# One held PSUM slot for both heads, an earlier start, earlier weights and an even product rate in a fused attention and feed-forward kernel

## The chip, the cores and the metric

The kernel runs on one core of a Trainium2 chip. The metric is the device time of one execution in microseconds (us). Engines are named as in the profile: PE (TensorE), DVE (VectorE), ACT (ScalarE), POOL (GpSimd), SP (the engine whose queue issues most transfers). A span is the time from the first to the last instruction of the profiled execution; an execution takes about 1.8 us more than its span (325.73 against 323.9 us). Each run also lists the mean clock that PE was granted (0.983 to 1.0 here), and that turns out to matter.

## The reference, cut to what matters

```python
# B, H, S, D = 4, 8, 768, 64; proj: 64 x 6
mask   = bucket(q) == bucket(k)          # six sign bits of q @ proj and k @ proj
scores = where(mask, q @ k.T / 8, -1e9)
attn   = softmax(scores) @ v             # per batch and head
x      = attn as (3072, 512)
h      = x @ w_in                        # 512 -> 2048
g      = h + sin(alpha * h)**2 / alpha
out    = g @ w_out                       # 2048 -> 512
```

There are 16 pairs of heads, four to a batch. A pair takes 12 steps: two heads, six blocks of keys.

## The kernel before

The parts that the change touches. `slot()` hands out two-bank pieces of PSUM in rotation, three in all; scores use them, and a slot taken with `hold=True` leaves two to the scores. Banks 6 and 7 hold the weighted values and the product of the last matrix.

```python
turns = deque(range(3))
def slot(hold=False):
    n = turns.popleft()
    if not hold:
        turns.append(n)
    return banks[:, 2 * n:2 * n + 2, :], n
```

A pair's q and k are prepared in parts during the pair ahead of it. For the first six pairs PE makes the transposed blocks:

```python
def prepare_on_pe(i):
    ...                                   # copies, hash, bits, picks; a yield after each part
    for h in range(2):
        if held is not None:
            give_back(held)
        ps, held = slot(hold=True)        # each head takes a slot
        for t in range(2):                # q, then k
            out = ps[0:KA, t, 0:HALF].bitcast(BF16)
            for s in range(SB):
                nc.tensor.transpose(out[:, s * 128:(s + 1) * 128], nat[:, s, 2 * t + h], ident)
            ...                           # DVE copies it out (once: ACT)
            yield
```

A step of attention issues the scores of one block of keys, its exponential on ACT, then `at_step` (parts of preparation, loads, product), then weighs by the values a block three steps old. When a head is weighed to its end, DVE computes `total`, a reciprocal and `xn` from bank 6, and from pair 5 on the next head weighs into the same bank.

```python
def fill(rate, most=3):                   # put some matmuls of the last product here
    nonlocal owed, rest
    owed += rate
    if rest:                              # the step after a finished tile places none,
        rest = False                      # while DVE copies the tile out of bank 7
        return
    while owed >= 1.0 and todo and most:
        owed -= 1.0
        most -= 1
        done = next(todo[0], None)        # one matmul; true if it finished a tile of 16
        if done is None:
            todo.popleft()
        if done:
            rest = True
            break
```

A batch is followed, one pair later, by its expansion (`x @ w_in`, sine, square: 16 chunks). Its product (96 matmuls, six tiles of 16) is then spread by `fill` over the four pairs that follow.

The softmax here doesn't subtract the row's maximum and nothing guards it: scores larger than these inputs give would overflow.

## Time and profile before

| what | before |
|---|---|
| runs known at the start | 326.29, 328.03 and 446.79 us (the last was the first execution) |
| median in the later calls, 9 to 11 runs each | 325.96 to 327.2 us |
| span of the profiled execution | 323.9 us |
| PE busy, ACT busy | 305.0 us (94%), 242.9 us (75%) |
| period of an early pair | 10.62 us |

### The profile page before, as it was taken

To read this page: it belongs to the slowest core of one execution; us is meant where nothing else is said; L and a number is where in the kernel's file an instruction comes from. 1 tells how busy PE (TensorE), PEld (TensorE's weight loads), DVE (VectorE), ACT (ScalarE), POOL (GpSimd) and SP (SyncE) were. 2 spreads that over 40 slices of the span, in tenths; PEclk is the share of its full clock that TensorE was granted. 3 is DMA by queue.
4 is the path that set the end of the run, shared out by engine and by line. 5 is a ranking of instruction groups with operands and counts; after the bars stand their busy time and mean duration, and the time that the engine had idled before them with its cause. 6 is when DMAs were issued, how large, how long until landed. Compare 5 with 4: busy or idle time off the path is not lost.

```text
span 323.9 us, 7681 instructions
## 1 busy us (share of the span) xinstructions
PE 305.0 (94%) x3059; PEld 183.3 (57%) x3059; DVE 196.7 (61%) x338; ACT 242.9 (75%) x298; POOL 94.6 (29%) x175
## 2 busy tenths in 40 slices
PE   6799999998989999989999999989999999899996
PEld 5566566664635556556645555656645655465444
DVE  4656546569864265569984466569984342499511
ACT  1387888888977778789988778789988888399200
POOL 5952642812883405051400605052300000000000
PEclk9799999999999999999999999999999999999999
DMA  7902576279965766869006476978003312200022
GB/s 257 328 4 60 183 235 191 72 207 257 376 235 144 159 172 152 232 109 200 0 2 195 113 213 106 223 125 192 2 9 92 66 71 59 57 2 0 4 113 81
DMA packets 68724, 42.87 MB, mean 132 GB/s; under 512 B 46560, under 2 KB 63696, under 8 KB 68688
## 3 DMA queue, kind: packets, MB, share of 16 engines
q1 hardware_dynamic: 68576, 42.37, 49.5%
q8 instruction: 24, 0.39, 0.5%
q14 instruction: 12, 0.10, 0.1%
q10 hardware_dynamic: 112, 0.01, 0.0%
HBM read 28.01 MB, written 7.27 MB: 109 GB/s over the span
## 4 chain that ended last, share of the span: by engine, by line
PE 66%; DMA 12%; DVE 6%; ACT 5%; POOL 5%; SPq 4%; issue 2%; ACTq 0%; DVEq 0%; POOLq 0%
PE banks L414 21%; PE banks L449 19%; PE banks L380 12%; PE banks L360 7%; ACT e L387 4%; PE banks L191 3%; PE banks L255 2%; DMA v_3064<-in_v_dram 2%; DMA k_150<-in_k_dram 2%; DMA v_3276<-in_v_dram 2%; SPq L92 2%; SPq L279 2%; DMA w_1467<-in_moe_w_in_dram 2%; DMA v_1090<-in_v_dram 1%; DMA w_1611<-in_moe_w_out_dram 1%
## 5 line engine op out<-in xcount | busy, mean ns | idle before, releaser
L387 ACT ACTIVATE e<-banks 128x768 bf16<-128x768 f32 x192 | 149.9, 810 | 36.7 <-PE banks L380 29.4
L449 PE MATMUL banks<-w_out_bf,g 128*128 128x512 bf16 (+1 forms) x400 | 102.1, 370 | 1.9 <-POOL w_out_bf L174 1.5
L380 PE MATMUL banks<-qa,ka 76*128 76x384 bf16 x384 | 94.2, 327 | 1.7 <-ACT e L387 1.4
L414 PE MATMUL banks<-xt,w_in_bf 128*128 128x384 bf16 x512 | 85.5, 326 | 2.2 <-POOL w_in_bf L174 1.2
L360 PEld LDWEIGHTS <-e 128*128 128x128 bf16 x1152 | 57.6, 97 | 35.4 <-issue 6.7
L414 PEld LDWEIGHTS <-w_in_bf 128*128 128x128 bf16 x512 | 49.5, 98 | 35.8 <-POOL w_in_bf L174 2.0
L360 PE MATMUL banks<-vaug,e 128*128 128x65 bf16 x1152 | 64.9, 193 | 2.0 <-DVE total L328 1.9
L423 ACT ACTIVATE s<-banks,alpha_sb 128x768 bf16<-128x768 f32 x64 | 57.2, 893 | 11.7 <-PE banks L414 10.9
L449 PEld LDWEIGHTS <-g 128*128 128x128 bf16 x400 | 38.7, 97 | 35.5 <-issue 3.7
L457 DVE COPY osb<-banks 128x512 f32<-128x512 f32 (+1 forms) x25 | 16.7, 668 | 30.4 <-PE banks L449 30.4
L328 DVE TENSOR_TENSOR total<-banks,base 128x390 f32<-128x390 f32 x20 | 11.2, 561 | 36.8 <-PE banks L360 36.7
L380 PEld LDWEIGHTS <-ka 76*128 76x128 bf16 x384 | 26.9, 99 | 6.1 <-issue 3.1
L208 POOL TENSOR_TENSOR vacc<-vacc,vaug 128x130 f32<-128x130 f32 x48 | 20.7, 431 | 3.8
L255 PE MATMUL banks<-ident,nat 128*76 128x128 bf16 x144 | 12.5, 231 | 4.2 <-ACT e L387 2.4
L255 PEld LDWEIGHTS <-nat 128*76 128x76 bf16 x144 | 11.0, 123 | 8.6 <-issue 3.7
L191 PE MATMUL banks<-qt,w_hash 128*32 128x192 f32 x128 | 13.7, 332 | 0.8 <-DVE qt L182 0.8
L191 PE MATMUL banks<-kt,w_hash 128*32 128x192 f32 x128 | 13.5, 332 | 0.3 <-DVE kt L182 0.3
L334 DVE TENSOR_TENSOR xn<-total,rden 128x384 bf16<-128x384 f32 x20 | 11.9, 597 | 0.7
L259 DVE COPY qa<-banks 76x768 bf16<-76x768 bf16 x12 | 6.6, 550 | 8.7 <-PE banks L255 8.7
L288 DVE TENSOR_SCALAR bits<-banks,side 128x192 bf16<-128x192 f32 x20 | 7.4, 412 | 5.5 <-ACT e L387 4.7
L191 PEld LDWEIGHTS banks<-qt,w_hash 128*32 128x32 f32 x128 | 6.0, 109 | 7.0 <-ACT e L387 2.5
L232 DVE TENSOR_SCALAR bit<-banks,bound 128x192 bf16<-128x192 f32 x6 | 2.5, 418 | 8.5 <-PE banks L191 8.5
(276 smaller groups left out, 290.5 us busy)
## 6 DMA issues: line engine op xcount, KB each, us to landing
out_dram<-osb SPq DMA_DIRECT2D x23, 256.0 KB
rows<-bits SPq DMA_DIRECT2D x40, 24.0 KB
w_663<-in_moe_w_in_dram SPq DMA_DIRECT2D x1, 512.0 KB
w_883<-in_moe_w_in_dram SPq DMA_DIRECT2D x1, 512.0 KB
w_1104<-in_moe_w_in_dram SPq DMA_DIRECT2D x1, 512.0 KB
w_1341<-in_moe_w_in_dram SPq DMA_DIRECT2D x1, 512.0 KB
w_1414<-in_moe_w_in_dram SPq DMA_DIRECT2D x1, 512.0 KB
w_1451<-in_moe_w_in_dram SPq DMA_DIRECT2D x1, 512.0 KB
```

The lines of the kernel that those rows point to most:

```text
L191: nc.tensor.matmul(out=ps[32 * j:32 * j + 32, 0:SB * 32].rearrange("p (s c) -> p s c", s=SB), lhsT=w_hash[:, blk].rearrange("p l a -> p (l ...
L208: nc.gpsimd.tensor_tensor(out=dst, in0=vacc[:, sb % 2], in1=vaug[:, :, sb], op=ALU.add)
L255: nc.tensor.transpose(out[:, s * 128:(s + 1) * 128], nat[:, s, 2 * t + h], ident)
L328: nc.vector.tensor_tensor(out=total, in0=cols, in1=operands[i][4][:, hh].unsqueeze(1).to_broadcast([128, SB, D + 1]), op=ALU.add,)
L334: nc.vector.tensor_tensor(out=xn[:, :, hh, :], in0=cols[:, :, 0:D], in1=rden.unsqueeze(2).to_broadcast([128, SB, D]), op=ALU.mult,)
L360: nc.tensor.matmul(out=regions[:, qb * (D + 1):(qb + 1) * (D + 1)], lhsT=e[:, qb * 128:(qb + 1) * 128], rhs=vaug[:, hh, kb, :], start=(apa ...
L380: nc.tensor.matmul(out=sc[:, half, 0:HALF], lhsT=ka[0:KA, hh, kb * 128:(kb + 1) * 128], rhs=qa[0:KA, hh, half * HALF:(half + 1) * HALF], s ...
L387: nc.scalar.activation(out=e.rearrange("p (h c) -> p h c", h=2), in_=sc[:, :, 0:HALF], func=AF.Exp, scale=SCALE,)
L414: nc.tensor.matmul(out=h[:, half, 0:HALF], lhsT=w_in_bf[:, p, F * 128:(F + 1) * 128], rhs=xt[b][:, p, half * HALF:(half + 1) * HALF], star ...
L423: nc.scalar.activation(out=s.rearrange("p (h c) -> p h c", h=2), in_=h[:, :, 0:HALF], func=AF.Sin, scale=alpha_sb[:, F:F + 1],)
L449: nc.tensor.matmul(out=o, lhsT=g[:, F, sub * 128:(sub + 1) * 128], rhs=w_out_bf[:, F, c0:c1], start=(F == 0), stop=(F == NF - 1),)
L457: nc.vector.tensor_copy(out=osb[:, c0:c1], in_=o)
```

## The change

Its intent: fewer waits of PE at each stage. The parts, as numbered in the prediction: (1) the start, (2) one held slot with steps moved by one, (3) weight pieces early, (4) an even product rate of 1.75, (5) a rate of 1.9 in the last three pairs.

```diff
         make_identity(nc, ident)
+        nc.gpsimd.tensor_copy(out=ident32, in_=ident[0:NF, 0:NF])           # (1)
 ...
-            for blk, engine in ((0, nc.vector), (1, nc.gpsimd)):
-                engine.tensor_copy(
+            for blk in range(2):
+                nc.gpsimd.tensor_copy(
                     out=w_hash[32 * a:32 * a + 32, blk, 0:NB, a], ...
     def invert_alpha():
-        nc.vector.tensor_copy(out=ident32, in_=ident[0:NF, 0:NF])
 ...
+        if held is not None:                                                # (2)
+            give_back(held)
+        ps, held = slot(hold=True)
         for h in range(2):
-            if held is not None:
-                give_back(held)
-            ps, held = slot(hold=True)
-            for t in range(2):
+            if (i, h) == (0, 1):
+                ps = banks[:, 6:8, :]
+            for t in ((1, 0) if i == 0 else (0, 1)):
 ...
-            at = [(0, n) for n in (1, 2, 4, 5, 7, 8, 8, 10)]
+            at = [(0, n) for n in (2, 3, 5, 6, 8, 9, 9, 11)]
-            at = [(i - 2, n) for n in (4, 7, 11)] + [(i - 1, n) for n in (1, 2, 3, 5, 6, 6, 8)]
+            at = [(i - 2, n) for n in (5, 7, 11)] + [(i - 1, n) for n in (1, 3, 4, 6, 7, 7, 9)]
 ...
-        for _ in range(3):                                                  # (1)
+        for _ in range(2):
             next(first)
         invert_alpha()
-        for _ in range(3):
+        for _ in range(4):
             next(first)
 ...
-                if n == 7 and 0 < i <= NPAIR:                               # (3)
-                    weigh_in(1 if i < NPAIR else 0)
-                fill(IN_ATTEND)                                             # was 2.0
+                if n in (8, 11) and 0 < i <= NPAIR:
+                    weigh_in(2)
+                fill(1.9 if i > n_pairs - NPAIR else 1.75)                  # (4), (5)
```

More of the change, by code (lines that the diff above doesn't have):

```diff
@@ L488, in drain @@
         owed, rest = 0.0, False
-    IN_ATTEND = 2.0
     n_pairs = len(pairs)
```

## The prediction

> **What bounds the kernel now.** I read the page first, then the times, then the waits of TensorE (PE) in total, then the timeline around each long one, and last the order of instructions of both kernels on each engine.
>
> The three runs are 446.79, 328.03 and 326.29 us. The first is far off and I drop it; the two others have a mean of 327.2, and the profiled execution took 325.73 with a span of 323.9. My base is 327.2.
>
> ```profile
> span 323.9 us, 7681 instructions
> PE 305.0 (94%) x3059; PEld 183.3 (57%) x3059; DVE 196.7 (61%) x338; ACT 242.9 (75%) x298; POOL 94.6 (29%) x175
> PE   6799999998989999989999999989999999899996
> PEclk9799999999999999999999999999999999999999
> ```
>
> PE is busy nearly everywhere, so it looks like the bound and leaves 324 - 305 = 19 us of idle time in all. But an early pair (the first five have no product to fill in) takes 10.6 us for 12 steps, and its steps without extra work follow each other in 0.51 us on PE (scores at 28.17 and 28.68); 12 x 0.51 plus the pair's hash, picks and 24 transposes (0.66 + 0.3 + 0.3 + 24 x 0.055) is some 8.7. In that part the 9s of the page are partly ends of matmuls that are only modelled, and stalls count more than the busy row says. The one low digit of the clock row is the slice at 8 to 16 us.
>
> The waits of PE, longest first:
>
> ```profile
> engine line waited for: us in total, times, longest us
> PE banks L255 <- ACT e L387: 2.4, 6, 0.4
> PE banks L360 <- DVE total L328: 1.9, 2, 0.9
> PE banks L449 <- POOL w_out_bf L174: 1.5, 3, 0.7
> ...
> PE banks L414 <- POOL w_in_bf L174: 1.2, 2, 0.7
> ...
> PE banks L153 <- DVE ident_105 L152: 1.2, 1, 1.2
> ...
> PE banks L414 <- DMA xt<-xn: 0.9, 1, 0.9
> ```
>
> Each of these six is a target of one part of the change; together 9.1 us. What the reader is to see: no single wait is large, and each sits in another stage. L255 is the block transposes, L360 the weighing by the values, L449 the last product, L414 the first product of the second half, L153 the transpose of alpha.
>
> The start, in order of time on VectorE (DVE), then on PE, then in the stretch from 11 to 12 us (busy time of PE, weight load, DVE, ACT and POOL, then the granted clock, 0.50, the DMA share and GB/s):
>
> ```profile
> 7.57 0.42 DVE L232 TENSOR_SCALAR bit<-banks,bound 128x192 bf16<-128x192 f32 x1 [0.95 <-PE banks L191]
> 7.90 0.78 DVE L152 CAST ident_105<-ident 16x16 f32<-16x16 bf16 x1
> 9.01 0.17 DVE L154 COPY alpha_sb<-banks 128x16 f32<-128x16 f32 x1 [0.32 <-PE banks L153]
> 9.21 0.49 DVE L155 TENSOR_SCALAR inv_alpha<-alpha_sb 128x16 f32<-128x16 f32 x1
> 9.74 0.25 DVE L156 RECIPROCAL inv_alpha<-inv_alpha 128x16 f32<-128x16 f32 x1
> 9.91 0.39 DVE L244 CAST nat<-banks 128x288 bf16<-128x288 f32 x1
> ```
> ```profile
> 10.46 2.55 PE L255 MATMUL banks<-ident,nat 128*76 128x128 bf16 x24 [1.23 <-POOL vaug L201]
> ```
> ```profile
> 11.00:12.00 1.00, 1.00 (x12) 1.00 (x11) 0.88 (x2) 0.23 (x1) 0.84 (x3) 0.50 1.08 378
> ```
>
> The bits are ready at 7.99, but four DVE instructions for alpha stand between them and the copy L244 that the transposes wait for; the picks on PE sit behind alpha's transpose too. The wait of L255 is put down to GpSimd (POOL); in program order that cast comes later, so it is L244. Then 24 transposes take 2.55 us, 106 ns each: the clock is at 0.50 from 11 to 14 us.
>
> [...] half clock for about three us, right after PE had been mostly idle from 7.5 to 10.4. [...] the 16x16 cast took 0.78 us and ended at 8.68, as the POOL cast that ran from 7.83 ended at 8.66; L155, 0.49 us for 16 columns, ended with the next POOL cast. [...]
>
> **The change part by part.** (1) Start. `ident32` is made by POOL beside the identity (near 1.5 us), alpha's transpose goes ahead of the hash on PE, and its three DVE instructions ahead of the bits, where DVE waited 0.95 for the hash. The eight copies into `w_hash` all go to POOL: 8 x 0.22 = 1.8 from 4.18, done at 6.0 in place of 5.07; DVE loses its four (0.70). The hash of k still needs k's transposed copy, bound by the landing of k near 5.7, so the hash ends near 7.4 as before. [...] bits start near 7.85, not 7.57. Then picks 8.3 to 8.6, L244 to 9.05, transposes at 9.15: 10.46 - 9.15 = 1.3 us earlier. The clock: half rate from 10.7 to 14 costs 3.3 / 2 = 1.6 us of PE's work; if the denser PE keeps the clock up it is saved. I give it 60%: 1.0. The casts of k for pair 1 land at 8.85 and stay ahead of need. Sum 2.3.
>
> (2) One held slot. Three slots of scores rotate and one is held. Before, the second head's transposes take another slot, whose exponential has to end first: in pair 2 PE waits 0.45 at 29.62 and 0.20 ahead of the next scores, then ScalarE (ACT) waits 0.63 for scores. Five pairs are prepared in this way during attention (1 to 5). Now head 1 uses head 0's slot, whose copies ended two steps (some 1.7 us) earlier. The first head still waits for a slot. 5 x 0.5 = 2.5, where 0.5 lies between PE's 0.45 and ACT's 0.63.
>
> (3) Eight weight pieces by pair 4 instead of four. The first expansion takes 67.14 to 91.1 us, 23.96, against 143.3 to 165.6, 22.3, for the second, which needs no weights. All eight pieces of the first matrix are loaded before it, the last two cast in its first two chunks; the eight of the second matrix follow in chunks of 1.4 us each at 1.4 us of transfer, done by chunk 11 of 16. Saves w_in 1.2 and w_out 1.5; but the first exponential after an expansion comes 4.59 us after its last matmuls start in both expansions, so part of w_out's wait is hidden: 2.4.
>
> (4) Product spread. 96 matmuls, 12 in the expansion, leave 84; at 2.0 a step they are used up with five steps left of 48. There PE runs 0.51 us steps and then stands 0.94 us for DVE's `total`, queued behind two stream transposes (1.9 us), once each in pairs 8 and 12. At 1.75, 84 / 48, the order of instructions shows two matmuls in the last step. A step with filler is 0.94 us, so the two steps between the DVE transposes and `total` cover them. 2 x (0.94 + 0.1 of small gaps) = 2.1.
>
> (5) Last batch. 1.9 instead of 2.0 over 36 steps: 16 matmuls, not 13, are left after the last weights, 3 x 0.215 = 0.65 against a wait of 0.94 for the last transposed block. 0.7.
>
> Sum 2.3 + 2.5 + 2.4 + 2.1 + 0.7 = 10.0. They lie in different stages on the path, so they add; I take off a tenth for what reappears as another small wait: 9.0. 327.2 - 9.0 = 318.2, put as 318.
>
> **The rivals.** (a) ACT becomes the bound of the early pairs. Against: its records follow each other 0.75 us apart (six in 4.51), 12 x 0.75 = 9.0 of 10.6. For: 12 x 0.81, the mean record, is 9.7, and with hash and picks on top part 2 would give 1 instead of 2.5: 320. (b) The start gains nothing: [...] the clock drops all the same: 320.5. Against: 1.3 us of DVE work leaves the path whatever the clock does. (c) Weight loads at steps 8 and 11 collide with the loads of q, k, v or POOL's casts, and an early pair waits: the DMA share is 0.33 to 0.64 from 30 to 66 us and POOL is busy about half, so four more casts of 1.04 us and 2 MB fit. If not, 1 to 3 us lost: 321. (d) An even spread leaves ACT short of scores instead: with 1.75 x 0.215 + 0.51 = 0.89 us a step PE stays slower than ACT's 0.81, so nothing is lost.
>
> **Range and chances.** Parts 3, 4 and 5 are read off as whole waits (5.2); 1 and 2 carry the doubt, 1.3 to 2.9 and 1 to 3. All low and a new wait gives about -6 (321.5); all high about -12.5 (314.5). 2% of 327.2 is 6.5, under the low end of most combinations: faster 0.85, same 0.14, slower 0.01.
>
> **What will show it.** Right: first transposes near 9.15 and first exponential before 12.2 (13.69 now); a clock row without the half-rate stretch (or with, then 1.6 worse); L255 waiting for ACT once, not six times, and early pairs of about 10.1 us; no waits for w_in; the first expansion near 22.3; no 0.94 wait for `total`; L414's wait for the last block gone. Wrong: pairs still 10.6 us with PE waiting for ACT elsewhere, POOL or the DMA queue ahead of PE in pairs 2 to 4, or DVE's `total` waits in other pairs.

## More of the kernel before

To compare stages I use the loads of ACT's function table, which part attention (exp) from expansion (sin). These are two of them in the timeline of ACT before; the columns are start, duration, engine, line and operation. Between them lies the second expansion, 23.37 us.

```profile
144.04 1.28 ACT L423 ACT_TABLE_LOAD   x1
...
167.41 1.28 ACT L387 ACT_TABLE_LOAD   x1
```

## The result, and the profile after

The median is 318.51 us (317.85 to 318.74, 4 runs) against 327.16 for the kernel before. The ratio is 0.9748, 95% interval 0.9698 to 0.9799. Ratios here are the mean time of one kernel's fast runs over that of the other's fast runs of the same rounds, so not quite the ratio of the medians. Executions over 1.5% slower than the fastest of the same kernel are left out of the means. A repetition (label e8_changed_again below) gave 318.85 and 0.9781. It was run at another time. The predicted time was 318.

The page after: span, busy time of the engines, PE's row and the row of its clock.

```profile
span 316.1 us, 7652 instructions
PE 301.7 (95%) x3029; PEld 184.3 (58%) x3059; DVE 196.0 (62%) x333; ACT 241.0 (76%) x298; POOL 94.4 (30%) x180
...
PE   7899999999999898999999899899999999999996
PEclk9999999999999999999999999999999999999999
```

The clock row has no low digit any more. The busy share of PE went from 94% to 95% and would not tell a reader that anything happened; it is also a little low after, where 30 records of the product are missing (x3029 against x3059). The waits of PE do (total us, times, longest):

```profile
PE banks L362 <- DVE total L330: 3.4, 4, 1.0
PE banks L382 <- ACT e L389: 1.1, 3, 0.4
...
PE banks L451 <- DVE osb L459: 0.6, 2, 0.3
...
PE banks L257 <- ACT e L389: 0.4, 1, 0.4
...
PE banks L416 <- DMA xt<-xn: 0.2, 1, 0.2
```

The waits for w_in and w_out are gone. The transposes (L257, which was L255) wait for ACT once instead of six times. The wait for the last transposed block fell from 0.9 to 0.2. But the wait for `total`, which part 4 was to remove, went up from 1.9 us in two places to 3.4 in four.

The table gives the length of each stage, worked out as differences of the start of the first exponential, of the table loads, of the first sine of the last expansion and of the span. Batches are named by the pairs in them.

| stage, us | before | after | difference | predicted, part |
|---|---|---|---|---|
| to the first exponential | 13.69 | 10.76 | -2.93 | -2.3 (1) |
| pairs 0 to 4 | 54.36 | 50.16 | -4.20 | -2.5 (2) |
| first expansion | 24.87 | 23.56 | -1.31 | -2.4 (3), with part of the next row |
| pairs 5 to 8 | 51.12 | 49.89 | -1.23 | and half of -2.1 (4) |
| second expansion | 23.37 | 23.74 | +0.37 | 0 |
| pairs 9 to 12 | 48.85 | 49.41 | +0.56 | half of -2.1 (4) |
| third expansion | 23.30 | 23.74 | +0.44 | 0 |
| pairs 13 to 15, to the last sine | 41.01 | 41.44 | +0.43 | -0.7 (5) |
| the rest | 43.33 | 43.40 | +0.07 | 0 |
| span | 323.9 | 316.1 | -7.8 | -10.0 before the deduction |

Each column is one trace. A second trace of the changed kernel (e8_changed_again) repeats the rows from pairs 5 on within 0.13 us, but its pairs 0 to 4 are 0.5 us longer and its first expansion 1.09 us longer (24.65), so the row of the first expansion is uncertain by about 1 us. And the 48.85 us of pairs 9 to 12 before is the lowest of all traces: four other kernels with the old rate have 49.28 to 49.41 there.

So the total came out as predicted while its terms did not. Two early ones gave more, and parts 4 and 5, for which I had counted 2.8 us of gain, show none. That is what the experiments are about.

My theory before them: the spread moves the step that rests after a finished tile. The order of instructions on PE in the changed kernel shows it. Here are steps 8 and 9 of pair 6 and steps 2 and 3 of pair 8; Q is the scores, cN are N product matmuls, V is the weighing, and the weighing of steps 9 and 3 is a head's first:

```
before:  pair 6, step 8   Q c3 V      step 9   Q c2 V
after:   pair 6, step 8   Q c1 V      step 9   Q    V      (rests)
before:  pair 8, step 2   Q c2 V      step 3   Q c2 V
after:   pair 8, step 2   Q c2 V      step 3   Q    V      (rests)
```

The same happens in pairs 10 and 12. These are the changed kernel's PE and DVE at step 3 of pair 8:

```profile
123.82 0.49 PE L382 MATMUL banks<-qa,ka 76*128 76x384 bf16 x2
125.18 0.34 PE L362 MATMUL banks<-vaug,e 128*128 128x65 bf16 x6 [0.87 <-DVE total L330]
```
```profile
123.84 0.69 DVE L459 COPY osb<-banks 128x512 f32<-128x512 f32 x1 [1.76 <-PE banks L451]
124.56 0.56 DVE L330 TENSOR_TENSOR total<-banks,base 128x390 f32<-128x390 f32 x1
```

A tile ended in the step in which a head ended. DVE copies the tile (0.69 us), then computes `total` (0.56 us). PE, with no product to place in this step, stands at the next head's first weighing, because it writes into the bank that `total` reads. The rival is that the spread is innocent and steps with a single product matmul (0.73 us in pair 6 of the changed kernel, from the scores at 100.53 us to the next at 101.26), shorter than ACT's exponential (0.81 us, the mean record), cost the time; or that its gain is there and hidden by something else.

### The profile page after: what moved, and what is told of

It is laid out like the page before. It is cut to its first block, busy times and chain, and to the rows that moved or that the text cites.

```text
span 316.1 us, 7652 instructions
## 1 busy us (share of the span) xinstructions
PE 301.7 (95%) x3029; PEld 184.3 (58%) x3059; DVE 196.0 (62%) x333; ACT 241.0 (76%) x298; POOL 94.4 (30%) x180
## 4 chain that ended last, share of the span: by engine, by line
PE 72%; DVE 9%; ACT 6%; DMA 5%; issue 3%; SPq 2%; POOL 1%; DVEq 0%; ACTq 0%; POOLq 0%
PE banks L416 23%; PE banks L451 19%; PE banks L382 15%; PE banks L362 9%; ACT e L389 4%; PE banks L191 3%; DVE g L403 3%; PE banks L257 2%; DMA v_3056<-in_v_dram 1%; DMA ka<-kn 1%; DMA k_145<-in_k_dram 1%; DVE total L330 1%; SPq L281 1%; ACT s L425 1%; DVE osb L459 1%
## 5 line engine op out<-in xcount | busy, mean ns | idle before, releaser
L389 ACT ACTIVATE e<-banks 128x768 bf16<-128x768 f32 x192 | 148.3, 811 | 33.8 <-PE banks L382 27.0
L451 PE MATMUL banks<-w_out_bf,g 128*128 128x512 bf16 (+1 forms) x370 | 98.1, 370 | 1.8 <-DVE osb L459 0.6
L425 ACT ACTIVATE s<-banks,alpha_sb 128x768 bf16<-128x768 f32 x64 | 57.1, 892 | 11.1 <-PE banks L416 10.2
L257 PEld LDWEIGHTS <-nat 128*76 128x76 bf16 x144 | 10.4, 114 | 3.6 <-issue 1.4
L257 PE MATMUL banks<-ident,nat 128*76 128x128 bf16 x144 | 11.5, 219 | 1.1 <-DVE nat L244 0.7
L201 POOL CAST vaug<-v_2847 128x768 bf16<-128x768 f32 x1 | 0.8, 830 | 25.4 <-DMA v_2847<-in_v_dram 25.4
```

The lines of the kernel that those rows point to most:

```text
L389: nc.scalar.activation(out=e.rearrange("p (h c) -> p h c", h=2), in_=sc[:, :, 0:HALF], func=AF.Exp, scale=SCALE,)
L425: nc.scalar.activation(out=s.rearrange("p (h c) -> p h c", h=2), in_=h[:, :, 0:HALF], func=AF.Sin, scale=alpha_sb[:, F:F + 1],)
L451: nc.tensor.matmul(out=o, lhsT=g[:, F, sub * 128:(sub + 1) * 128], rhs=w_out_bf[:, F, c0:c1], start=(F == 0), stop=(F == NF - 1),)
```

## The experiments

Twelve runs were made, one of them the changed kernel again; all were correct. "Before" is the kernel before on the same chip. By a threshold of 2% on the interval, e1, e7 and e9 to e12 are faster than before, e3 and e8 are unclear, and e2, e4, e5 and e6 count as the same; what they say about single parts rests on traces and on differences of a few us.

| run | median us | before | ratio (95% interval) |
|---|---|---|---|
| e1_rate_back | 316.41 | 327.2 | 0.9668 (0.9621 to 0.9715) |
| e2_rate_only | 327.41 | 327.2 | 0.9992 (0.9949 to 1.0034) |
| e3_slot_only | 320.21 | 327.2 | 0.9763 (0.9718 to 0.9807) |
| e4_start_only | 325.66 | 327.2 | 0.9909 (0.9835 to 0.9983) |
| e5_weights_only | 324.48 | 325.96 | 0.9949 (0.991 to 0.9987) |
| e6_steps_only | 323.51 | 325.96 | 0.9946 (0.989 to 1.0002) |
| e7_rest_moved | 317.23 | 325.96 | 0.9738 (0.9713 to 0.9762) |
| e8_changed_again | 318.85 | 325.96 | 0.9781 (0.9755 to 0.9808) |
| e9_tail_filled | 316.92 | 326.9 | 0.9686 (0.964 to 0.9732) |
| e10_even_but_last | 317.69 | 326.9 | 0.9708 (0.9662 to 0.9754) |
| e11_copy_on_act | 319.04 | 326.9 | 0.9745 (0.9694 to 0.9796) |
| e12_loads_earlier | 315.75 | 326.62 | 0.9671 (0.9639 to 0.9704) |

### The old rate in the changed kernel

```diff
-                fill(1.9 if i > n_pairs - NPAIR else 1.75)
+                fill(2.0)
```

> The changed kernel with only the rate of the product put back to 2.0 in every step. The prediction's parts 4 and 5 (the even spread saves 2.8) ask for 318.5 + 2.8 = 321.3. My theory after the two traces: the spread costs, because the step that rests after a finished product tile now falls on the first weighing of a head in pairs 6, 8, 10 and 12, and PE waits 3.4 us in all for DVE's total behind the copy of the tile, where the kernel before waited 1.9; the three stretches of pairs behind the expansions took 0.7, 1.0 and 0.4 us more than their share. It asks for 316.4, with two waits for total of 0.9 again and none of the four.

It took 316.41 us, where my theory had said 316.4 and the prediction's terms 321.3. Parts 4 and 5 cost about 2 us. The two old waits for `total` are back (1.9 us in two places), and so is the wait of 0.9 for the last block, and still it is faster than the changed kernel. The stages behind the pairs agree: 23.31 and 23.42 for the second and third expansion, 41.01 for the last pairs up to the sine. Pairs 5 to 8 take 49.33 instead of 49.89 us. Pairs 9 to 12 take 49.41 in both: here the old rate has a wait of 0.9 for `vsum`, a sum over v that POOL makes, in place of what it saves. PE's waits for ACT's exponentials are 1.1 us in three places in both kernels, which speaks against the rival of the short steps. The later repetition of the changed kernel, 318.85, keeps the distance; their ratios (0.9668 and 0.9781) stand apart. They were run at other times.

### The new rates in the kernel before

```diff
-                fill(IN_ATTEND)
+                fill(1.9 if i > n_pairs - NPAIR else 1.75)
```

> The kernel before with only the new rates. The prediction: 2.8 us faster than the kernel before. My theory: about 2 us slower, with four waits for total in pairs 6, 8, 10 and 12. A third view, that the spread costs only together with the faster early part, would give no difference.

The median is 0.2 us above that of before, ratio 0.9992: no gain, which refutes the term, but it does not show the 2 us of loss either. The waits are the ones of the theory:

```profile
PE banks L360 <- DVE total L328: 3.5, 4, 1.1
```

The stages behind the first expansion are longer by 0.48, 0.37, 0.66, 0.43 and 0.43 us in its trace, 2.4 together. The timed runs show less. Part of the gap goes with the clock: nine of the eleven runs of before had a mean clock of 0.983 to 0.995; of the six runs of this kernel, two had 1.0 and three 0.993 to 0.995, and the sixth, at 0.984, took 331.81 us and counts as slow. Among runs at 0.993 to 0.995, three of this kernel took 327.08 to 327.55 and two of before 326.09 and 326.82, some 0.8 us apart. So the size of the loss on this side stays between 0 and 2.4 us.

### The slot alone

Only part 2 of the diff, on the kernel before.

> The kernel before with only the one held slot and its shifted steps. The prediction gave 2.5 us for it (0.5 a pair). The traces say 4.2 for the five pairs (10.6 to 9.6 us each in the steady ones), so 4 to 5 us faster if the slot alone does it; 2.5 if half of it came from the start or from the weights.

It took 320.21 us, 7.0 below the median of before: most of the whole change. In the trace pairs 0 to 4 take 50.05 us instead of 54.36, 4.3 less (4.9 less than the 54.94 of the new rates on the old slots, a trace without a half-rate stretch). The rest of the difference of the medians goes in part with the clock: all four runs had 1.0, against 2 of 11 of before at 0.999 or above. To see where the 4.3 comes from, look at ACT in an early pair. First the kernel before, then the changed kernel (the slot alone gives the same lines at other times); in brackets is ACT's idle time before the group:

```profile
30.90 4.51 ACT L387 ACTIVATE e<-banks 128x768 bf16<-128x768 f32 x6 [0.63 <-PE banks L380]
35.81 2.22 ACT L387 ACTIVATE e<-banks 128x768 bf16<-128x768 f32 x3 [0.40 <-PE banks L380]
38.37 0.81 ACT L387 ACTIVATE e<-banks 128x768 bf16<-128x768 f32 x1 [0.34 <-PE banks L380]
39.38 1.51 ACT L387 ACTIVATE e<-banks 128x768 bf16<-128x768 f32 x2 [0.20 <-PE banks L380]
```
```profile
31.63 9.02 ACT L389 ACTIVATE e<-banks 128x768 bf16<-128x768 f32 x12 [0.58 <-PE banks L382]
```

Twelve exponentials run in one piece of 9.02 us, and one bubble of 0.58 us is left of four that summed to 1.57. The period is 9.02 + 0.58 = 9.60 us, against 10.62 (from 30.90 to the next group of six at 41.52). The early pairs are paced by ACT: each bubble of ACT counts in full, 1.57 - 0.58 = 0.99 us a pair. The gap of 0.63 us came back in every early pair of the kernel before, as a head took a second slot (before the groups at 21.50, 30.90, 41.52, 52.14 and 62.76 us), and is not in the changed kernel's piece above.

### The shifted steps alone

```diff
-            at = [(0, n) for n in (1, 2, 4, 5, 7, 8, 8, 10)]
+            at = [(0, n) for n in (2, 3, 5, 6, 8, 9, 9, 11)]
-            at = [(i - 2, n) for n in (4, 7, 11)] + [(i - 1, n) for n in (1, 2, 3, 5, 6, 6, 8)]
+            at = [(i - 2, n) for n in (5, 7, 11)] + [(i - 1, n) for n in (1, 3, 4, 6, 7, 7, 9)]
```

> The kernel before with only the steps of the preparation shifted, each head still in its own slot. The slot with its shift was worth 1.0 us a pair, 7 us in the median, where I had predicted 0.5 and 2.5. If the exchange of slots is the cost, this gives nothing; if a part comes from the shift, 1 to 3 us. The half-rate stretches that the kernel before shows in most runs should stay if the shift alone does nothing.

```profile
35.35 5.29 ACT L387 ACTIVATE e<-banks 128x768 bf16<-128x768 f32 x7 [0.58 <-PE banks L380]
41.27 3.80 ACT L387 ACTIVATE e<-banks 128x768 bf16<-128x768 f32 x5 [0.63 <-PE banks L380]
45.65 0.81 ACT L387 ACTIVATE e<-banks 128x768 bf16<-128x768 f32 x1 [0.58 <-PE banks L380]
```

The period is 45.65 - 35.35 = 10.30 us. So the shift takes 0.32 us off the period and the common slot, on top of it, the other 0.70, nearly all of it the 0.63 bubble that stays here. The common slot without the shift was not run. The median is 2.5 us below that of before, with an interval that reaches 1. All four runs have clocks of 0.990 to 0.995: the half-rate stretches stay with the shift alone, and one more of them comes up in this trace far from the start (last section).

### The start alone

Only part 1 of the diff, on the kernel before.

> The kernel before with only the start: ident32 and the w_hash copies on POOL, alpha ahead of the bits. The prediction: 1.3 us from the shorter DVE queue, and 1.6 more if the clock stays up, which it did in the changed kernel, where the first exponential came 2.9 us earlier. If clock and queue are the cause: 2.5 to 3 us faster with no half-rate stretch; if the clock was saved by the denser transposes of the one slot, 1.3 and a half-rate stretch remains.

Neither outcome that I had written down fits. The first exponential starts at 10.92 us, 2.8 earlier than in the profile of before. But the trace of the new rates on the old start (above), which had no half-rate stretch, already had it at 11.96, and the slot alone at 11.88. So the shorter queue is worth about 1.0 us, and the other 1.8 in my pair of traces goes with the clock of the one execution that was profiled. Some of the latter is lost again in the early pairs: at the start of the first expansion the three traces stand at 68.05 (before), 66.90 (new rates) and 65.85 us (this run), 1.15 for the clock and 1.05 for the queue. The median is 1.5 us below before, with one slow run in it; the fast runs give the ratio 0.9909, about 3.0 us, with an interval from 0.6 to 5.4. The chain behind it is as predicted; this is DVE in the changed kernel, then PE's transposes:

```profile
5.34 0.98 DVE L182 STREAM_TRANSPOSE kt<-k_145 128x768 f32<-128x768 f32 x1 [0.51 <-DMA k_145<-in_k_dram]
...
6.41 0.70 DVE L155 TENSOR_SCALAR inv_alpha<-alpha_sb 128x16 f32<-128x16 f32 x1
7.14 0.25 DVE L156 RECIPROCAL inv_alpha<-inv_alpha 128x16 f32<-128x16 f32 x1
```
```profile
8.77 1.50 PE L257 MATMUL banks<-ident,nat 128*76 128x128 bf16 x24 [0.70 <-DVE nat L244]
```

Alpha fills the time in which DVE used to wait for the hash (0.95 us in the kernel before), and the 24 transposes start at 8.77 where I had said 9.15. L155 is again long (0.70 us for 16 columns, 0.49 in the kernel before) and ends at 7.11, beside a POOL cast that ran from 6.26 to 7.08; that the cast holds it up is not shown.

### The weights alone

Only part 3 of the diff, on the kernel before.

> The kernel before with only the eight early weight pieces. The prediction: 2.4 us faster, the waits for w_in (1.2) and w_out (1.5) gone, the first expansion at 23.5 us between its table loads instead of 24.9. A loss of up to 1 us in pairs 2 to 4 if the loads collide.

It took 324.48 us, ratio 0.9949. In the trace the first expansion takes 23.31 us, 1.56 less, pairs 0 to 4 take as long as before (54.30), and the pairs behind the expansion 0.44 less. That is 2.0 where I had 2.4, with no collision in pairs 2 to 4. One pair of traces is thin here, since the first expansion alone varies: 23.99 to 26.22 us in the five traces without the early pieces, 23.31 to 24.65 in the nine with them. Together with pairs 5 to 8 it is steadier: 75.99 to 76.91 in the four traces without them at the old rate, 73.99 here and 73.13 in the changed kernel with the rate put back, so 2.0 to 3.8 less. A wait of 1.4 us for POOL's `vsum` turns up instead, which the last experiment takes up.

### The rest moved away from a head's first weighing

The even rates stay. On the step ahead of a head's first weighing, no tile is finished:

```diff
-    def fill(rate, most=3):
+    def fill(rate, most=3, first_weigh_next=False):
 ...
         while owed >= 1.0 and todo and most:
+            if first_weigh_next and into == NF - 1:   # into: matmuls of the tile so far
+                break
 ...
-                fill(1.9 if i > n_pairs - NPAIR else 1.75)
+                fill(1.9 if i > n_pairs - NPAIR else 1.75, first_weigh_next=n in (2, 8))
```

> The changed kernel once more, so that it shares chip and runs of before with the next one. 318.5 again; the first run with the old rates gave 316.4 on another call, and if that gap is real this one stays 2 us above it.

> The changed kernel with its even rates, and one rule more: on the step ahead of a head's first weighing no product tile is finished, so that the step that rests never is the one that weighs first. If the four waits for total (3.4 us) are the cost of the spread, they go, and it falls to 315 to 316. If they only move PE's slack about, it stays at 318.5. If steps with a single product matmul, faster than ACT's exponential, are the cost, it stays near 318 without the waits.

The changed kernel again took 318.85 us and this one 317.23, 1.6 less. The intervals of their ratios overlap slightly (up to 0.9762 and from 0.9755), but the runs themselves lie apart: 317.05 to 317.62 against 318.11 to 319.36. PE's waits in it:

```profile
PE banks L382 <- ACT e L389: 1.8, 3, 0.6
PE banks L362 <- DVE total L330: 1.3, 3, 0.6
...
PE banks L451 <- DVE osb L459: 1.0, 4, 0.3
```

The wait for `total` fell from 3.3 to 1.3 us, and 1.1 us of other waits (ACT and the tile copy) came up. In the traces, pairs 5 to 12 take 98.10 us here and 99.30 in the changed kernel. So the coincidence of tile end and head end is a cause, and worth 1.2 to 1.6 us; it is not the whole of the cost, since 317.2 is still above the old rate's 316.4. It was run at another time. The traces say where the rest is: pairs 5 to 12 are now 0.6 us shorter than the 98.74 of the old rate, which has the 0.9 for `vsum` among them, but the second and third expansion together are 0.75 longer, and the last pairs to the sine 0.6 (41.58 against 41.01). So whether the even spread gains anything in its pairs stays open.

### The last three pairs put back

```diff
-                fill(1.9 if i > n_pairs - NPAIR else 1.75)
+                fill(2.0 if i > n_pairs - NPAIR else 1.75)
```

> The changed kernel with 2.0 in the last three pairs and the even 1.75 kept elsewhere: part 5 alone undone. The prediction gave part 5 a gain of 0.7, so this would be 319.5; by the stretches of the trace the last batch lost 0.4 net, so 318.3, with the stretch of pairs 13 to 15 back at 35.1 us from 35.8 and the 0.9 wait for the last block back.

It took 317.69 us, below the changed kernel's 318.51 and 318.85. They were run at other times. Pairs 13 to 15 are back at 35.09 us from 35.80, and with the way to the sine the stage takes 41.00 instead of 41.44. The wait for the last block is 0.9 again. So part 5 removed the wait that it aimed at, and the three pairs ahead of it took 0.7 us longer, which is more than the three matmuls moved out of them were worth. In those pairs of the changed kernel PE waited 0.32 and 0.24 us for DVE's tile copy behind a rest.

### The tile copy on ACT

```diff
-                nc.vector.tensor_copy(out=osb[:, c0:c1], in_=o)
+                if last:
+                    nc.vector.tensor_copy(out=osb[:, c0:c1], in_=o)
+                else:
+                    nc.scalar.copy(out=osb[:, c0:c1], in_=o)
```

> The changed kernel as it is, even rates included, with the copies of finished product tiles of the first three batches on ACT instead of DVE. If the four waits for total come from DVE doing the tile copy (0.69) ahead of total, as the order in the queue suggests, they shrink to 0.1 each and the time falls by 2 to 3 us, to 316; if ACT becomes late with the scores' exponentials, PE waits for ACT instead and nothing is won. If the waits stay, the tile copy isn't their cause.

```profile
PE banks L451 <- ACT osb L462: 2.1, 3, 0.7
PE banks L362 <- DVE total L330: 1.8, 4, 0.8
```

It took 319.04 us: nothing won. The wait for `total` halves, from 3.4 to 1.8, in four places still, so the copy ahead of `total` made half of it and the chain of `total` itself the other half. What was won there is lost as PE waits for the tile copy in ACT's queue. I had expected the waits to shrink to 0.1 each; they did not.

### The last pair of a batch filled at the old rate

At 2.0 the product ends five steps before its batch. Its last 13 matmuls are dealt over pair 8 and pair 12 so that the steps at the head's end have some:

```diff
-                fill(2.0)
+                fill((0.0, 1.0, 1.0, 1.0, 1.0, 1.0, 2.0, 2.0, 2.0, 1.0, 2.0, 2.0)[n]
+                     if i in (2 * NPAIR, 3 * NPAIR) else 2.0)
```

> The changed kernel at the old rate of 2.0, with the 13 matmuls that the last pair of a batch has left (pairs 8 and 12) dealt one a step and two in steps 6 to 8, so that its heads' ends have work beside them and no tile ends there. That run had 316.4 and two waits of 0.94 for total. If those waits were the worth that I gave the even spread (part 4), they go and it falls by 1 to 1.9 us, to about 315; if steps with one matmul are bound by ACT and give it back, it stays at 316.4.

It took 316.92 us, no better than the rate put back (in another call). The wait for `total` fell from 1.9 to 0.6 as meant. PE now waits in pairs 8 and 12 for `vsum`; of these 1.9 us the rate put back had 0.9 already, in pair 12:

```profile
PE banks L302 <- POOL vsum L208: 1.9, 2, 1.3
...
PE banks L362 <- DVE total L330: 0.6, 1, 0.6
```

### Loads four steps earlier

```diff
-                if n == 6 and i + 3 < n_pairs:
+                if n == 2 and i + 3 < n_pairs:
                     load(i + 3)
```

> The run with the filled last pair (rate 2.0), which had 316.9 although its waits for total fell from 1.9 to 0.6 us, with the loads of q, k and v issued at step 2 of a pair instead of step 6. That run had 1.9 us of new waits of PE for POOL's vsum in pairs 8 and 12 (1.26 and 0.65), where POOL had waited for v. If v was issued too late, behind the stores of product tiles in the same queue, those waits go and it falls to 315; if v lands late for another cause, it stays at 316.9.

It took 315.75 us (314.28 to 316.25, all six runs at clock 1.0), 1.2 below the run without it, which was in another call, and no wait for `total` is left. One wait for `vsum` of 0.8 remains, at another instruction, and PE waits 2.1 us for ACT instead of 1.1. That the waits of 1.9 went fits v having been issued late. This is the fastest kernel, below both the kernel before and the changed kernel. Its ratio (0.9671) is that of the rate put back (0.9668); that it beats that one is likely by the medians and not shown.

## Why the prediction was right or wrong

The total was right, 318 for 318.5. It was right because errors of its terms cancelled, and that is luck. The stated range was no safer: with the highest values given for parts 1 and 2 its terms sum to 5.2 + 2.9 + 3 = 11.1, not 12.5.

Part 1, 2.3 us, of which 1.3 from the queue and 1.0 as 60% of 1.6 from the clock. The queue was worth 1.0 to 1.6 at the first exponential (11.88 and 11.96 on the old start at a granted clock of 1.00, 10.39 to 10.92 in nine traces of the new), so 1.3 was sound. The clock term was right to be a chance; its 60% was my estimate, and no run shows that a denser PE keeps the clock up, or that the term belongs to part 1. The stretch at half rate is not a property of the old kernel: of the five traces with the old start, three have it and two don't. 17 of 42 runs of the kernel before had a mean clock of 0.998 or more; of the kernels with both the new start and the one slot, 42 of 44. The start alone had 3 of 4, the slot alone 4 of 4, the shift and the weights alone 0 and 1 of 4. So a mean clock below 0.998 came in 2 of 44 runs of the kernels with both and in 25 of 42 of the kernel before; why, no run tests, and which part does most stays open with so few runs.

Part 2, 2.5 us: the mechanism was right, the size too small. The failed term is "5 x 0.5 = 2.5, where 0.5 lies between PE's 0.45 and ACT's 0.63". The common slot measured 0.70 a pair on top of the shift of the steps, and the shift, which I had given nothing, 0.32. The pairs came to 9.60 us where I had said about 10.1. I had the fact in hand that the early pairs are not bound by PE and then still averaged PE's wait with ACT's. On the engine that paces the stage the bubbles are to be summed: 1.57 before. Rival (a) was right that ACT becomes the bound (9.02 of 9.60 us), but its cost of 12 x 0.81 was too high; the twelve follow each other 0.75 apart, as its own counterargument had it.

Part 3, 2.4 us: 2.0 in the trace of the weights alone, 2.0 to 3.8 across traces. The step held within that spread. Two details of it were off: the second expansion starts at 143.14 and not 143.3, so the first was 1.5 longer and not 1.7, and the last two pieces of `w_in` were cast at 67.2 and 70.7 us, well after the first two chunks, without a wait of PE.

Part 4, 2.1 us: wrong in sign. The failed step is "so the two steps between the DVE transposes and `total` cover them. 2 x (0.94 + 0.1 of small gaps) = 2.1". The two waits that it spoke of did go. What I left out is that a rate also sets where tiles end. Six rests move with it, and in the order of instructions that I had before me one fell on a head's first weighing in pairs 6, 8, 10 and 12. I had read that order only for its last steps. Rival (d) asked whether ACT would run short and said that nothing is lost; the loss was on DVE, which no rival named, though the last of the signs of being wrong, "DVE's `total` waits in other pairs", did, and it came true.

Part 5, 0.7 us: the wait of 0.94 fell to 0.24 as worked out, but the stage grew by 0.4, since the pairs ahead grew by 0.7.

Parts 4 and 5 together: some 2 us lost for 2.8 expected. Against the trace of the rate put back, the two traces of the changed kernel lose 0.5 to 0.6 in pairs 5 to 12, 0.75 to 0.9 in the second and third expansion and 0.4 in the last pairs. Moving the rests more than covers the first (1.2 in the traces). Why the expansions are longer stays open: they take 23.73 to 23.87 us in the five traces with the even rate and the tile copy on DVE, against 23.31 and 23.42 at the rate put back. My reading, that the changed kernel still has product in the steps before and the old rate has ACT caught up, is argued, not shown.

The tenth taken off "for what reappears as another small wait" was right in kind: waits for `vsum` and for ACT came up in run after run as others went.

## What to carry to other kernels

Work that is spread over a loop to fill holes brings its own ends with it, and each end takes an engine for a while (here DVE, 0.69 us for the copy of a tile); before changing the rate, list where the ends fall against the moments at which that engine is needed by something else. Where a stage is paced by an engine, add up that engine's bubbles over one period, before and after (here ACT's, 1.57 and 0.58 us), rather than the waits of the busiest one. And a total that comes out right is no evidence for its terms: compare stage by stage, and undo the terms one at a time.

## What the traces and runs show of the granted clock

- The shift alone (e6_steps_only) fell to half rate in mid-run, from about 214.5 to 217.9 us by the shares of its slices. From 211 to 214 us PE had been busy for 1.46 of 3.00 us, at a granted clock of 1.00; in the kernel before, from 7.5 to 10.4 us, ahead of its stretch at 0.50, for 0.51 of 2.90 us. The columns are the stretch, its length, busy time of PE, weight load, DVE, ACT and POOL, then the granted clock, DMA share and GB/s:

```profile
211.00:212.00 1.00, 0.22 (x7) 0.21 (x7) 0.93 (x4) 1.00 (x2) 0.86 (x3) 1.00 0.85 87
212.00:213.00 1.00, 1.00 (x23) 0.48 (x18) 0.55 (x1) 0.78 (x2) 0.90 (x2) 1.00 0.11 22
213.00:214.00 1.00, 0.24 (x8) 0.10 (x1) 0.28 (x1) 0.36 (x1) 0.84 (x3) 1.00 0.25 70
214.00:215.00 1.00, 0.61 (x8) 0.50 (x8) 0.75 (x3) 0.00 (x0) 1.00 (x2) 0.74 0.60 217
215.00:216.00 1.00, 1.00 (x9) 0.63 (x8) 0.00 (x0) 0.32 (x1) 0.87 (x2) 0.50 0.24 82
```

- In the kernel before, 24 transposes took 2.55 us from 10.46 us on, 106 ns each, and the granted clock was 0.50 from 10.7 to 14 us; in the changed kernel 24 transposes took 1.50 us, 62 ns each, at a granted clock of 1.00.
- Of the kernel before, 25 of 42 runs had a mean clock below 0.998, and in the third call its fast runs at 0.990 and below took 327.3 to 329.5 us where those at 0.999 and above took 325.0 to 326.8 (one run at 0.995 took 329.6, so not all of it goes with the clock): enough to blur a change of one per cent.
